# A delta-rule recurrence with a mixture-of-depths block on one core: four matmul tiles side by side, queries turned late, keys loaded once, table blocks interleaved by two

## The chip, the core and the metric

The kernel runs on one core of one Trainium2 chip. Time is device time in microseconds (us) from the launch's first to its last instruction, the median of several executions; lower is better. Five engines work beside each other, each strictly through its own list of instructions: TensorE (PE; its weight loads are PEld), VectorE (DVE), ScalarE (ACT), GpSimd (POOL) and SyncE (SP), which here only issues DMAs. An instruction that waits on one engine holds up everything behind it on that engine.

## The reference

Four batches, eight heads, 768 tokens, head dimension 48. Per head a 48x48 state is read and updated token by token (delta rule), and the heads' outputs side by side are rows of 384 numbers. Then, per batch, the 128 rows with the highest score go through a two-layer network and are added back with a gate.

```python
k_n = k / (np.linalg.norm(k, axis=-1, keepdims=True) + 1e-06)
for t in range(S):
    kt, vt, bt = (k_n[:, :, t], v[:, :, t], beta[:, :, t, None])
    y[:, :, t] = np.einsum('bhd,bhde->bhe', q[:, :, t], state)
    v_old = np.einsum('bhde,bhd->bhe', state, kt)
    state = state + bt[:, :, :, None] * np.einsum('bhd,bhe->bhde', kt, vt - v_old)
# x: (B, S, H*D)
scores = np.einsum('bsd,d->bs', x, w_gate)
out = x.copy()
for b in range(B):
    top_idx = np.argpartition(-scores[b], capacity)[:capacity]   # capacity 128
    xe = x[b, top_idx]
    ye = np.maximum(xe @ w1, 0.0) @ w2                           # 384 -> 1024 -> 384
    g = 1.0 / (1.0 + np.exp(-scores[b, top_idx]))
    out[b, top_idx] = x[b, top_idx] + g[:, None] * ye
```

## The kernel before

**Chunks.** The tokens are cut into chunks of 64, so that a chunk's 64 updates become matmuls and one triangular inverse. Batches go in two groups of two (16 heads, in 8 pairs); a group has 12 chunks, one after the other, and the two groups follow each other: 24 steps i.

**Per step.** `prep(i)` loads keys and queries, turns both on TensorE (L431), copies them out (ACT, L435), and multiplies keys by keys and keys by queries in one matmul of 128 columns (L448); ACT copies the results (L457) to `g` and `p`, and POOL masks `p` (L465). `recur(i)` is the chain through the state: `mm_r` (keys times the old state, L682), `sub` on DVE (L686), `mm_w` (inverse times right side, L694), `out_w` on ACT twice (L700), `mm_s` (new state, L708), `out_s` on ACT (L714); beside it `mm_q` (queries times state, L721), `mm_p` (L731), the copy to `x` (L737), the store to `out` (L744) and the scores (POOL L749, ACT L756).

**Per four steps.** `eliminate(e)`, e = 0 to 5, inverts the triangles of four chunks. On 128 partitions lie 128 blocks' halves: DVE turns the table in (L536), ACT takes a root (L542), DVE makes scales (L546 to L551), multiplies the table (L561), ACT copies it to PSUM (`fill`, L566), and then DVE does 29 working pairs of a product (L575) and a subtraction (L579), each step needing the one before; a closing multiplication (`final`, L585) and two transposes, `turn_out` to `tt` (L589) and `turn_back` to `g` (L594). A DMA on SP moves half of `tt` (`mv`, L600), and `join` makes the other half with small matmuls (`z` L635, `jj` L646). Only then can `mm_w` of those four steps start.

**Per batch.** `depths(b)` spreads the scores (L837), counts for each token how many are larger (compares L870 to L881, on POOL for batches 0, 1 and 3, on DVE for batch 2; count matmuls L894), picks the 128 row numbers (`choose` L913, `mm_idx` L920 in fp32), gathers the rows, and runs the two layers (L951, L965), gate (L970) and scatter (L974).

**What sets the order.** All work is given to `Plan` with an engine, an assumed duration, what it needs and a priority; `Plan` makes every engine's list from that before the program is built. Nothing is reordered on the chip. Where its plan leaves TensorE little to do, `Plan.fill` puts in a filler: two bf16 matmuls of ones (L1055) whose result nobody reads. SP's list holds all loads but a few early ones, and the stores.

Of tiles: a matmul of at most 64 rows and 64 columns takes a quarter of TensorE's array. The rows are chosen by the input's partitions (0 or 64 on), the columns by the output's. `mm_r` goes through the four combinations in the order `par_rt`; `mm_w` and `mm_q` use two of them, with the same number for rows and columns:

```python
nc.tensor.matmul(pw[half[par], a % 2, a // 2],                       # mm_w
                 lhsT=tt[half[par], ch * GP + a], rhs=x[half[par], a], ...)
y[half[rt], (2 * a + par) * D:(2 * a + par + 1) * D]                 # mm_q, output
lhsT=kq[ds[rt], a, 1, half[par]], rhs=s_old[ds[rt], a, par]          # mm_q, inputs
```

Of the kernel before, what the change touches and what calls it, by code (L numbers as in the profile page):

```python
# [20 lines left out]
class Op:  # L21
    __slots__ = ("eng", "dur", "emit", "deps", "prio", "take", "give", "lat",
                 "start", "end", "left", "users", "seq")


class Plan:
# [56 lines left out]
    def fill(self):  # L83
# [5 lines left out]
        for op in ops + [None]:  # L89
            end = op.start if op else last  # L90
            while t + 0.15 < end:
                if any(a < t < b for a, b in used):
                    t += 0.1
                    continue
                near = sum(min(y, t) - max(x, t - 3.4) for x, y in work[-40:] if y > t - 3.4)
                if near < 2.4:
                    fill = Op()
                    fill.eng, fill.start, fill.end, fill.give, fill.seq = "PE", t, t, [], -1
                    fills.append(fill)
                    work.append((t, t + 0.3))  # L100
                t += 0.3
            if op:
                work.append((op.start, op.end))
                t = max(t, op.end)
# [86 lines left out]
def kernel(  # L191
# [33 lines left out]

    nc = tc.nc
# [21 lines left out]
    SPARE = (10, 11)  # L248
# [15 lines left out]
    ring("k", 3, [GP, DP])  # L264
    ring("ks", 4, [GP, D])
    ring("q", 3, [GP, DP])
    ring("v", 3, [GP, D])
    ring("kq", 12, [GI, 2, P])
    ring("p", 12, [GP, C])
    ring("g", 2, [NB, C])  # L270
    ring("a", 1, [HC, HC])
    ring("mb", 1, [HC, HC])
    ring("tt", 2, [NB, C])
    ring("x", 2, [GB, DM // 2])
    ring("xw", 1, [GB, DM // 2])
    ring("rep", 2, [NT, P])
    ring("sel", 1, [NT, P])
    ring("cmp", 1, [22 * P], BF16)
# [3 lines left out]
    ring("oe", 1, [DM])  # L282
# [12 lines left out]
    def maker(eng):  # L295
        def add(dur, emit, deps=(), prio=0.0, take=(), give=(), lat=0.15):
            return plan.add(eng, dur, emit, deps, prio,
                            [(t[0] if isinstance(t, tuple) else t, t) for t in take],
                            give, lat)
        return add  # L300
# [3 lines left out]
    def moved(eng, dur, size, emit, deps=(), prio=0.0, take=(), give=(), lat=1.9):  # L304
# [6 lines left out]
    beta_src = beta.rearrange("(g bb) (r par) (e c half t) -> par half g e c (bb r) t",  # L311
                              bb=GB, par=2, half=2, t=HC, c=BC)

    def load_beta(eng, e):
        for par in range(2):
            for half in range(2):
                p0 = (par * 2 + half) * HC
                eng.dma_start(out=bt[p0:p0 + HC, e],
                              in_=beta_src[par, half, e // (NCH // BC), e % (NCH // BC)])
# [5 lines left out]
    tok = [sbuf(f"tok{b}", [NT, 2]) for b in range(B)]  # L325
    wg = sbuf("wg", [DM // 2])
    fold = sbuf("fold", [C])
# [4 lines left out]
    spare = w1_sb.rearrange("p t f -> p (t f)")  # L332
    w = GI * 2 * P
    rings["kq2"] = [spare[:, m * w:(m + 1) * w].rearrange("p (r o t) -> p r o t", o=2, t=P)
                    for m in range(2)]
    plan.ring("kq2", 2)
    w = GP * C
    rings["p2"] = [spare[:, 4 * w + m * w:4 * w + (m + 1) * w]
                   .rearrange("p (r t) -> p r t", t=C) for m in range(2)]
    plan.ring("p2", 2)  # L340
    rings["g2"] = [w2_sb.rearrange("p f d -> p (f d)")[:, :NB * C]
                   .rearrange("p (n t) -> p n t", t=C)]
# [8 lines left out]
    junk = sbuf("junk", [DM // 2], BF16)  # L351
    sc = [sbuf(f"sc{b}", [NCH]) for b in range(B)]
# [4 lines left out]
    def constants():  # L357
# [3 lines left out]
        for t in rings["k"][:4] + rings["q"] + rings["k"][4:]:  # L361
            nc.vector.memset(t[:, :, D:], 0.0)
        make_identity(nc, ident)
# [3 lines left out]
        load_beta(nc.gpsimd, 0)  # L367
# [8 lines left out]
        for b in range(B):  # L376
            nc.gpsimd.iota(tok[b][:, :, 0], pattern=[[P, NT]], base=b * S,
                           channel_multiplier=1, allow_small_or_imprecise_dtypes=True)
        nc.vector.tensor_tensor(out=fold, in0=ident[:, :C], in1=ident[:, C:], op=ALU.add)

    def load_w(what, t):
        if what == 0:
            step = list(moe_w_gate.ap[0])[0]
            for rt in range(2):
                nc.sync.dma_start(out=wg[half[rt]], in_=bass.AP(
                    tensor=moe_w_gate.tensor, offset=moe_w_gate.offset + 2 * D * rt * step,
                    ap=[[0, C], [4 * D * step, HP // 2], [step, 2 * D]]))
# [10 lines left out]
    par_rt = [(0, 0), (1, 1), (0, 1), (1, 0)]  # L398
    half = [slice(par * C, (par + 1) * C) for par in range(2)]
    lo = [slice(par * C, par * C + HC) for par in range(2)]  # L400
    hi = [slice(par * C + HC, (par + 1) * C) for par in range(2)]
    ds = [slice(rt * DP, rt * DP + D) for rt in range(2)]

    def load(i, nm, eng=None):
        g, c = divmod(i, NCH)
        eng = eng or nc.sync

        def emit():
            t = got(nm, i)
            for par in range(2):  # L410
                eng.dma_start(
                    out=t[half[par], :, :D],
                    in_=src[nm[0]][par, c * C:(c + 1) * C, g * GP:(g + 1) * GP])
# [4 lines left out]
    def gk(e):  # L418
        return "g2" if e == 2 else "g"

    def kk(i):
        return "kq2" if i in SPARE else "kq"

    def pk(i):
        return "p2" if i in SPARE else "p"

    def turn(i, o, nm):
# [6 lines left out]
        def out():  # L434
            nc.scalar.copy(got(kk(i), i)[:, :, o],  # L435
# [3 lines left out]
    def bank(i, w, rt):  # L439
        return got("inv", i, w, rt).rearrange("p (r o t) -> p r o t", o=2, t=C)  # L440

    def products(i, n, w, o):
# [643 lines left out]
```

## Time and profile before

| | |
|---|---|
| median of 3 runs | 365.71 us (361.34 to 366.37) |
| the profiled execution | 365.55 us |
| its span, first to last instruction | 363.7 us |
| mean granted TensorE clock | 0.809 of full |
| busy: PE / PEld / DVE / ACT / POOL | 311.0 / 267.2 / 212.5 / 168.8 / 173.4 us |
| matmul instructions | 6156 |

A busy share says how long an engine had something under way, not that it ran at its peak or that anything waited for it. The granted clock has two levels, 1.2 GHz (0.50 in the rows) and 2.4 GHz (1.00); a stretch between them was part at one and part at the other. The page's own chain of waits covers just the last 16 us, the closing of the program, so the limits are read from the engines' timelines. The three stretches used below are: up to the first `out_w`, from there to the last, and the rest.

### The profile page before, as it was taken

Reading aid. Unit: us, or ns where it says so; the run is one execution under the profiler, and the core shown is the slowest. Engines: PE = TensorE matmul, PEld = TensorE weight load, DVE = VectorE, ACT = ScalarE, POOL = GpSimd, SP = SyncE. Lnnn points to the kernel's source line nnn. Section 1 sums busy time; section 2 is a strip of 40 time slices with the busy share of each in tenths; the row PEclk is TensorE's granted clock in tenths of the full one; section 3 lists DMA queues with packets and bytes.
Section 4 is the critical chain, followed back from the end, with each engine's and each line's share of the span. In section 5 each row is a group of like instructions: output and inputs, shape, how many; then the busy total and the mean of one; then the engine's idle time right before and its main releaser. Section 6 shows DMA issues by size and latency. Waiting matters only on the chain. (4 is left out here: it accounts for less than half of the span.)

```text
span 363.7 us, 14373 instructions
## 1 busy us (share of the span) xinstructions
PE 311.0 (86%) x6156; PEld 267.2 (73%) x6156; DVE 212.5 (58%) x538; ACT 168.8 (46%) x453; POOL 173.4 (48%) x221
## 2 busy tenths in 40 slices
PE   6797679998759997998947897989999998988992
PEld 5575558887649875987837777879899787858781
DVE  5159995799918699769938897696542512301000
ACT  1476635666154585565646554443344552211121
POOL 6026426013543126334297549885694287393111
PEclk9999965799555798589968996785555999995998
DMA  9467767476453345645584845243130120111011
GB/s 120 93 132 138 136 118 125 78 137 129 74 113 81 76 98 106 128 87 118 118 208 120 198 95 98 58 83 78 42 54 23 47 48 22 14 31 22 23 22 22
DMA packets 139678, 31.92 MB, mean 88 GB/s; under 512 B 137488, under 2 KB 139040, under 8 KB 139616
## 3 DMA queue, kind: packets, MB, share of 16 engines
q1 hardware_dynamic: 134432, 28.64, 39.8%
q0 software_dynamic: 960, 1.59, 2.6%
q10 hardware_dynamic: 4224, 0.79, 1.5%
q8 instruction: 48, 0.79, 0.9%
q14 instruction: 14, 0.11, 0.1%
HBM read 22.61 MB, written 5.51 MB: 77 GB/s over the span
## 5 line engine op out<-in xcount | busy, mean ns | idle before, releaser
L575 DVE TENSOR_TENSOR tmp<-a,pa 128x30 f32<-128x30 f32 (+9 forms) x180 | 58.9, 327 | 21.2 <-ACT pa L566 15.7
L579 DVE TENSOR_TENSOR pa<-pa,tmp 128x30 f32<-128x30 f32 (+9 forms) x180 | 60.8, 338 | 6.2
L674 POOL TENSOR_TENSOR v<-v,nnT 128x384 f32<-128x384 f32 x24 | 20.8, 867 | 82.3 <-DMA v<-in_v_dram 50.7
L870 POOL TENSOR_SCALAR cmp<-rep,tok 128x256 bf16<-128x256 f32 (+5 forms) x42 | 46.5, 1119 | 7.5 <-PE inv L894 7.4
L749 POOL TENSOR_TENSOR xw<-x,wg 128x384 f32<-128x384 f32 x23 | 23.2, 1011 | 33.3 <-ACT x L737 12.6
L465 POOL TENSOR_SCALAR_AFFINE_SELECT p<-p 64x512 f32<-64x512 f32 x44 | 28.8, 654 | 18.0 <-ACT p L457 16.5
L448 PE MATMUL inv<-kq 48*64 48x128 f32 (+1 forms) x832 | 32.4, 288 | 5.6 <-ACT kq L435 2.7
L694 PE MATMUL prec<-r,tt 64*64 64x48 f32 x704 | 31.2, 245 | 4.7 <-ACT tt L651 3.0
L694 PEld LDWEIGHTS prec<-r,tt 64*64 64x64 f32 x704 | 28.0, 159 | 8.1 <-ACT tt L651 3.4
L700 ACT COPY wbd<-prec 64x384 f32<-64x384 f32 x48 | 22.7, 473 | 22.5 <-PE prec L694 17.8
L448 PEld LDWEIGHTS inv<-kq 48*64 48x64 f32 x832 | 25.2, 155 | 10.6 <-ACT p L457 3.7
L721 PE MATMUL inv<-s,kq 48*64 48x48 f32 x640 | 30.6, 258 | 1.6 <-ACT w_sb L640 1.6
L435 ACT COPY kq<-inv 128x512 f32<-128x512 f32 x44 | 24.8, 591 | 15.0 <-DMA q<-in_q_dram 8.6
L951 PEld LDWEIGHTS inv<-xeT,w_sb 128*128 128x128 f32 x192 | 26.6, 208 | 5.1 <-ACT xeT L945 1.1
L721 PEld LDWEIGHTS inv<-s,kq 48*64 48x64 f32 x640 | 28.2, 174 | 3.0 <-ACT w_sb L640 1.7
L951 PE MATMUL inv<-xeT,w_sb 128*128 128x128 f32 x192 | 27.9, 295 | 0.0
L708 PE MATMUL psta<-wbd,ks 128*48 128x96 f32 x352 | 24.2, 294 | 3.2 <-ACT wbd L700 3.2
L651 ACT COPY tt<-inv 32x256 f32<-32x256 f32 x48 | 17.3, 361 | 19.4 <-DMA tt<-tt 14.2
L686 DVE TENSOR_TENSOR r<-v,prec 128x384 f32<-128x384 f32 x22 | 12.1, 551 | 23.9 <-PE prec L682 12.7
L731 PE MATMUL inv<-wbd,p 128*64 128x96 f32 x352 | 25.1, 301 | 1.1 <-POOL p L465 1.0
L965 PE MATMUL inv<-w_sb,hT 128*128 128x384 f32 x64 | 25.4, 500 | 0.0
L708 PEld LDWEIGHTS psta<-wbd,ks 128*48 128x48 f32 x352 | 19.2, 149 | 6.4 <-ACT wbd L700 4.7
(112 smaller groups left out, 551.8 us busy)
## 6 DMA issues: line engine op xcount, KB each, us to landing
v<-in_v_dram SPq DMA_DIRECT2D x48, 96.0 KB
out_dram<-x SPq DMA_DIRECT2D x96, 48.0 KB
k<-in_k_dram SPq DMA_DIRECT2D x44, 96.0 KB
q<-in_q_dram SPq DMA_DIRECT2D x44, 96.0 KB
ks<-in_k_dram SPq DMA_DIRECT2D x44, 96.0 KB
tt<-tt SPq DMA_DIRECT2D x12, 128.0 KB
w_sb<-in_moe_w_dram SPq DMA_DIRECT2D x4, 384.0 KB
w_sb<-in_moe_w_dram SPq DMA_DIRECT2D x3, 512.0 KB
```

The costliest lines, as they stand in the source:

```text
L435: nc.scalar.copy(got(kk(i), i)[:, :, o], got("inv", i, nm).rearrange("p (r t) -> p r t", t=P))
L448: nc.tensor.matmul(bank(i, w, rt)[half[par], r, o], lhsT=kq[ds[rt], r, 0, half[par]], rhs=kq[ds[rt], r, o, half[par]], start=True, stop=True)
L465: nc.gpsimd.affine_select(out=t[half[par]], in_=t[half[par]], pattern=[[0, GP], [1, C]], base=0, channel_multiplier=-1, compare_op=ALU.is_ ...
L575: nc.vector.tensor_tensor(out=t, op=ALU.mult, in0=a[:, j + 1:, j:j + 1].to_broadcast([P, w, j]), in1=x[:, j:j + 1, :j].to_broadcast([P, w, ...
L579: nc.vector.tensor_tensor(out=x[:, j + 1:, :j], in0=x[:, j + 1:, :j], in1=t, op=ALU.subtract)
L694: nc.tensor.matmul(pw[half[par], a % 2, a // 2], lhsT=tt[half[par], ch * GP + a], rhs=x[half[par], a], start=True, stop=True)
L708: nc.tensor.matmul(psta[ds[a % 2], a // 2], lhsT=t[:, a, :D], rhs=wb[:, a].rearrange("p h d -> p (h d)"), start=(c == 0 and a < 2), stop=True,
L721: nc.tensor.matmul(y[half[rt], (2 * a + par) * D:(2 * a + par + 1) * D], lhsT=kq[ds[rt], a, 1, half[par]], rhs=s_old[ds[rt], a, par], star ...
L731: nc.tensor.matmul(y[half[a % 2], (a // 2) * 2 * D:(a // 2 + 1) * 2 * D], lhsT=t[:, a], rhs=wb[:, a].rearrange("p h d -> p (h d)"), start= ...
L870: eng.tensor_scalar(out=cmp[:, at + x * P:at + y * P], in0=rows[:, x * P:y * P], scalar1=mine, scalar2=None, op0=op)
L951: nc.tensor.matmul(got("inv", b, "h", f // 2)[:, f % 2 * CAP:(f % 2 + 1) * CAP], lhsT=w1_sb[:, t, f * P:(f + 1) * P], rhs=got("xeT", b)[:, ...
L965: nc.tensor.matmul(got("inv", b, "o")[:CAP, :DM], lhsT=got("hT", b)[:, f], rhs=w2_sb[:, f], start=(f == 0), stop=(f == KF - 1))
```

## The change

What it does, part by part:

- `mm_q` and `mm_w` go through all four combinations of row half and column half (list `four`). For that the value side puts the batch of a group, and not the parity of the head, on the partition half, and `y` is spread over two banks.
- Keys by keys (`products_g`) and keys by queries (`products_p`) become separate matmuls of 64 columns, since their outputs now lie by different bits of the head. Queries are loaded and turned later (own rings `qT`, 7, and `kT`, 12).
- `mm_s` reads the keys that were loaded for turning (ring `k`, 12): the second load of the keys (`ks`) goes. Scores and stores take whole rows of 384: one store a step for four, one score for two. All `beta` loads go to POOL, at the start.
- Tables `g` and `tt` hold two blocks interleaved, so their transposes and shift DMAs see pairs of neighbouring numbers.
- In `eliminate`, two `a` tables; for e of 1 and more the scaling runs on POOL, and the mask is applied before it (`clear`), not after it by a table.
- Compares run on DVE for batches 1 to 3; `mm_idx` is bf16 with the numbers split in three parts.
- `Plan.fill` weighs TensorE's work by a rate and fills more often: 139 fillers for 44.

```diff
+    ring("k", 12, [GP, DP])
...
+    ring("kT", 12, [GI, P])
+    ring("qT", 7, [GI, P])
...
+    ring("a", 2, [HC * HC])
+    ring("tt", 2, [NB // 2, C, 2])
...
+    four = [(0, 0), (1, 1), (0, 1), (1, 0)]
...
+    def products_g(i):
+            t = got("kT", i)
+            for k in range(2):
+                for par in range(2):
+                    for rt, bb in four:
+                        x = t[ds[rt], 2 * bb + k, half[par]]
+                        nc.tensor.matmul(small(i, "g", rt)[half[bb], k, par], lhsT=x, rhs=x,
+                                         start=True, stop=True)
...
         def mm_w():
-            for a in range(GP):
-                for par in range(2):
-                    nc.tensor.matmul(pw[half[par], a % 2, a // 2],
-                                     lhsT=tt[half[par], ch * GP + a],
-                                     rhs=x[half[par], a], start=True, stop=True)
+            for m in range(GP // 2):
+                for bb, par in four:
+                    nc.tensor.matmul(pw[half[par], bb, m], lhsT=tt[half[bb], m, par],
+                                     rhs=x[half[bb], 2 * m + par], start=True, stop=True)
...
+            for k in range(2):
+                for par in range(2):
+                    for rt, bb in four:
+                        nc.tensor.matmul(
+                            y(rt)[half[bb], k, par], lhsT=t[ds[rt], 2 * bb + k, half[par]],
+                            rhs=s_old[ds[rt], 2 * bb + k, par],
+                            start=(k == 0 and par == 0), stop=False, skip_group_check=True)
...
+        eng, on = (nc.vector, dve) if e == 0 else (nc.gpsimd, pool)
...
+        last = on(0.35, square, [s["in"]], u)
+        cl = pool(1.5, clear, [last], u)
+        s["rt"] = act(0.3, root, [last], -600)
+        s["nn"] = dve(0.85, norms, [s["rt"], N.get(("e", e - 2), {}).get("fi")], u)
+        s["sc"] = on(0.6, scales, [s["nn"]], u)
+        last = on(1.4 if e == 0 else 2.2, scale, [s["sc"], cl], u)
         last = act(1.0, fill, [last], -600, take=[("A", e)])
         for j in range(1, HC - 1):
             emit, dur = step(j)
-            last = dve(dur, emit, [last], u)
+            last = dve(dur, emit, [last, N.get(("e", e - 1), {}).get("tb")], u)
...
-        on, eng = (dve, nc.vector) if b == 2 else (pool, nc.gpsimd)
+        on, eng = (dve, nc.vector) if b >= 1 else (pool, nc.gpsimd)
...
-                if near < 2.4:
+                if near < 2.8 and (t > 3.4 or t + 0.12 < end):
```

How the lists change at two places. First DVE, where the first elimination ends (`a_100` and `a_107` its table, `g_99` and `g_106` the table of the second elimination). Before:

```order
L585 TENSOR_TENSOR a_100<-pa,mb_101 128x1024
L589 STREAM_TRANSPOSE tt_102<-a_100 128x32x32
L594 STREAM_TRANSPOSE g_98<-a_100 128x32x32
L536 STREAM_TRANSPOSE a_100<-g_99 128x1024
L538 TENSOR_SCALAR nrm<-a_100 128x32
L546 TENSOR_SCALAR nrm<-nrm 128x32
L548 RECIPROCAL bh_141<-nrm 128x32
L549 TENSOR_TENSOR bh_141<-bh_141 128x32
L550 TENSOR_TENSOR bh_141<-bh_141,bt 128x32
L551 STREAM_TRANSPOSE nnT_138<-nrm 128x32
L561 TENSOR_TENSOR a_100<-a_100,bh_141 128x1024
L563 MEMSET a_100 128x32
```

With the change:

```order
L612 TENSOR_TENSOR pa<-pa,tmp 128x3x28
L577 TENSOR_SCALAR nrm<-nrm 128x32
L579 RECIPROCAL bh_155<-nrm 128x32
L580 STREAM_TRANSPOSE nnT_152<-nrm 128x32
L608 TENSOR_TENSOR tmp<-a_107,pa 128x58
L612 TENSOR_TENSOR pa<-pa,tmp 128x2x29
L608 TENSOR_TENSOR tmp<-a_107,pa 128x30
L612 TENSOR_TENSOR pa<-pa,tmp 128x30
L618 TENSOR_TENSOR a_107<-pa,bh_154 128x16x2x32
L624 STREAM_TRANSPOSE tt_109<-a_107 128x32x16x2
L630 STREAM_TRANSPOSE g_105<-a_107 128x32x16x2
L608 TENSOR_TENSOR tmp<-a_108,pa 128x30
```

The second elimination's preparation has moved ahead of the first one's end (its transpose in stands eight instructions above the first row shown), its multiplications and the clearing have gone to POOL, and the first step of the second elimination follows `turn_back` at once.

Second SP, around the first `mv` (`tt_102` and `tt_109`). Before:

```order
L411 DMA v_73<-in_v_dram 64x8x48 x2
L411 DMA ks_66<-in_k_dram 64x8x48 x2
L411 DMA k_62<-in_k_dram 64x8x48 x2
L476 DMA w_sb<-w_sb 32x16x32 x2
L411 DMA k_63<-in_k_dram 64x8x48 x2
L600 DMA tt_102<-tt_102 32x32x32 x2
L411 DMA q_68<-in_q_dram 64x8x48 x2
L476 DMA w_sb<-w_sb 32x16x32 x2
L411 DMA q_70<-in_q_dram 64x8x48 x2
L318 DMA bt<-in_beta_dram 32x1x32 x4
```

With the change:

```order
L400 DMA w_sb<-in_moe_w_dram 128x1024 x2
L425 DMA q_74<-in_q_dram 64x8x48 x2
L425 DMA q_75<-in_q_dram 64x8x48 x2
L425 DMA q_73<-in_q_dram 64x8x48 x2
L637 DMA tt_109<-tt_109 32x16x64 x2
L422 DMA v_76<-in_v_dram 64x8x48 x2
L425 DMA k_61<-in_k_dram 64x8x48 x2
L794 DMA out_dram<-x_111 2x64x384
```

The `ks` and `bt` issues are gone from SP (208 DMAs in all for 337), the keys of twelve chunks stand ahead of all else, and weights of the network are loaded before the first `mv`.

## Rows read from the trace of the kernel before

**Rows 1.** A window of ten us: span, busy us (instructions) of each engine, granted clock, DMA share, GB/s
```profile
270.00:280.00 10.00, 10.00 (x196) 9.44 (x196) 1.35 (x4) 5.64 (x19) 4.95 (x6) 0.50 0.08 23
```
**Rows 2.** Timeline of ACT, `fill` of the first and last elimination: start, us, instruction
```profile
26.19 1.02 ACT L566 COPY pa<-a 128x1024 f32<-128x1024 f32 x1 [0.47 <-DVE a L563]
...
227.24 1.02 ACT L566 COPY pa<-a 128x1024 f32<-128x1024 f32 x1 [0.23 <-DVE a L563]
```
**Rows 3.** Timeline of DVE, between eliminations: first end, fourth end, last end
```profile
49.33 1.23 DVE L585 TENSOR_TENSOR a<-pa,mb 128x1024 f32<-128x1024 f32 x1
...
175.50 1.96 DVE L589 STREAM_TRANSPOSE tt<-a 128x1024 f32<-128x1024 f32 x1
177.32 2.14 DVE L594 STREAM_TRANSPOSE g<-a 128x1024 f32<-128x1024 f32 x1
...
179.49 1.97 DVE L536 STREAM_TRANSPOSE a<-g 128x1024 f32<-128x1024 f32 x1
...
256.07 1.23 DVE L585 TENSOR_TENSOR a<-pa,mb 128x1024 f32<-128x1024 f32 x1
```
**Rows 4.** The page's costliest groups, the two operations of the elimination's steps
```profile
L575 DVE TENSOR_TENSOR tmp<-a,pa 128x30 f32<-128x30 f32 (+9 forms) x180 | 58.9, 327 | 21.2 <-ACT pa L566 15.7
L579 DVE TENSOR_TENSOR pa<-pa,tmp 128x30 f32<-128x30 f32 (+9 forms) x180 | 60.8, 338 | 6.2
```
**Rows 5.** Waits of DVE: who waited for whom, us in total, times, longest
```profile
DVE tmp L575 <- ACT pa L566: 15.7, 5, 7.6
DVE r L686 <- PE prec L682: 12.7, 7, 3.2
```
**Rows 6.** Timeline of SP's queue around the fourth `mv`
```profile
179.55 2.30 SPq L391 DMA_DIRECT2D w_sb<-in_moe_w_dram  x2
181.95 1.37 SPq L600 DMA_DIRECT2D tt<-tt  x2
```
**Rows 7.** Timeline of ACT, `out_w`: first step, two in mid program, last step
```profile
64.11 0.96 ACT L700 COPY wbd<-prec 64x384 f32<-64x384 f32 x2
...
195.44 0.96 ACT L700 COPY wbd<-prec 64x384 f32<-64x384 f32 x2
...
214.79 0.96 ACT L700 COPY wbd<-prec 64x384 f32<-64x384 f32 x2 [1.17 <-PE prec L694]
...
296.94 0.96 ACT L700 COPY wbd<-prec 64x384 f32<-64x384 f32 x2 [1.05 <-PE prec L694]
```
**Rows 8.** Timeline of PE at full clock: `mm_q`, `mm_r`, `mm_w`
```profile
166.59 1.10 PE L721 MATMUL inv<-s,kq 48*64 48x48 f32 x32
...
171.92 0.68 PE L682 MATMUL prec<-s,w_sb 48*64 48x48 f32 x32
...
173.55 1.13 PE L694 MATMUL prec<-r,tt 64*64 64x48 f32 x32
```
**Rows 9.** Timeline of PE at half clock: `mm_r`, `mm_q`, three fillers
```profile
260.38 1.10 PE L682 MATMUL prec<-s,kq 48*64 48x48 f32 x32 [0.58 <-ACT s L714]
261.27 1.91 PE L721 MATMUL inv<-s,kq 48*64 48x48 f32 x32
263.11 0.82 PE L1055 MATMUL psta<-warm 128*128 128x128 bf16 x6
```
**Rows 10.** Timeline of PE at full clock, products of 128 columns
```profile
29.28 1.10 PE L448 MATMUL inv<-kq 48*64 48x128 f32 x32
```
**Rows 11.** Lines of PE by form, 20 to 35 us, products of 64 columns
```profile
L448 PE MATMUL inv<-kq 48*64 48x64 f32 x64 | 1.5, 225 | 0.0
```
**Rows 12.** Lines by form, whole span: `mm_idx`, and POOL's `beta` loads
```profile
L920 PE MATMUL inv<-tok,sel 128*128 128x2 f32 x48 | 9.4, 323 | 0.0
...
L318 POOL DMA_DIRECT2D bt<-in_beta_dram x4 | 2.6, 653 | 0.3 <-issue 0.3
```
**Rows 13.** Timeline of DVE, last count of batch 3
```profile
328.94 0.16 DVE L906 TENSOR_TENSOR count<-count,inv 128x4 f32<-128x4 f32 x1 [10.91 <-PE inv L894]
```
**Rows 14.** Waits of POOL: for the values' load
```profile
POOL v L674 <- DMA v<-in_v_dram: 50.7, 12, 9.0
```

More of the change, by code (lines that the diff above doesn't have):

```diff
@@ L324 @@
     tri = sbuf("tri", [P])
-    tok = [sbuf(f"tok{b}", [NT, 2]) for b in range(B)]
-    wg = sbuf("wg", [DM // 2])
-    fold = sbuf("fold", [C])
+    own = [sbuf(f"own{b}", [NT]) for b in range(B)]
+    tok = [sbuf(f"tok{b}", [NT, 2, 3], BF16) for b in range(B)]
+    part = sbuf("part", [NT])
+    both = [sbuf(f"both{b}", [2]) for b in range(2)]
+    wg = sbuf("wg", [DM])
     warm = sbuf("warm", [P], BF16)
@@ L509, in prep @@
[L509 removed]
+        for w, v, made, deps, rate in (
+                ("g", u, (products_g, split_g), [n["ek"], N[e * BC].get("g")], 1.2),
+                ("w", u + 31, (products_p, split_p), [n["ek"], n["eq"]], 1.2)):
             keys = [("inv", i, w, rt) for rt in range(2)]
[L511 to L521 removed]
@@ L522, in prep @@
-        n["mp"] = pool(1.4, mask_p(i), [n["e", 1, 0], n["e", 1, 1]], 10 * i - 10)
-        done = [n["e", 0, 0], n["e", 0, 1]]
-        if first:
-            n["sh"] = dve(0.85, shift0(i), done, u)
+            n[w] = pe(0.52, made[0](i), deps, v, rate=rate,
+                      take=keys + ([("p", i)] if w == "w" else
+                                   [gk(e)] * (i % BC == 0)))
+            for rt in range(2):
+                n[w, rt] = act(0.37, made[1](i, rt), [n[w], n.get((w, 0))], v,
+                               give=[keys[rt]])
@@ L602, in eliminate @@
-        s["in"] = dve(2.2, turn_in, [N[i].get("sh") for i in range(e * BC, (e + 1) * BC)],
+            left, right = lower(got("tt", e), slice(0, NB // 2))
+            for x in range(2):
+                nc.sync.dma_start(out=left[lo[x]], in_=right[lo[x]])
+        s["in"] = dve(1.3, turn_in, [N[i].get("sh") for i in range(e * BC, (e + 1) * BC)],
                       u, take=[("a", e)])
-        s["rt"] = act(0.3, root, [s["in"]], -600)
-        s["sc"] = dve(1.0, scales, [s["rt"], N.get(("beta", e)),
-                                    N.get(("e", e - 2), {}).get("mb")], u)
@@ L765, in recur @@
+        r["w"] = pe(0.52, mm_w, [x, n["ej"], s_mv(e), o.get("w0"), o.get("w1")], u, rate=1.5,
+                    give=[("tt", e)] + ([("v", i)] if c == 0 else []))
+        for par in range(2):
+            r[f"w{par}"] = act(0.45, out_w(par),
+                               [r["w"], prev2.get("p"), prev2.get("s")], u)
+        ready = [r["w0"], r["w1"]]
         if c < NCH - 1:
-            n["ls"] = moved(sp, 1.3, 1.15, load(i, "ks"), prio=10 * i - 24, take=[("ks", i)])
-        r["vh"] = pool(1.05, vh, [n["lv"], N["e", e]["sc"]], u - 8)
@@ L791, in recur @@
+        xo = None
+        for rt in range(2):
+            xo = act(0.37, out_x(rt), [r["p"], xo], 10 * i + 8, take=[("x", i)] * (rt == 0),
+                     give=[yk[rt]])
         how = dve if i == NU - 1 else act
```

580 lines of the change are left out of this document (283 added, 297 removed).

## The prediction, made before the changed kernel ran

> **What bounds the kernel now.** I read the page's busy shares first and trusted none: TensorE is under way 86% of the span, but a mean granted clock of 0.809 says that much of that is slow running. The windows show it best: from 270 to 280 us TensorE is busy 10.00 of 10 us at a clock of 0.50, the lower of its two levels, while DVE has 1.35 us of work [rows 1]. There TensorE is the limit, and slow. Earlier it is not alone. The timelines cut the span in three by `out_w` [rows 7]: 64.1 us to the first, 232.8 us to the last (296.94), 66.8 us for what is left.
>
> In the middle stretch DVE's eliminations set the pace. The first `fill` starts at 26.19 us, the sixth at 227.24 [rows 2]: (227.24 - 26.19)/5 = 40.2 us each. The steps' own two operations take (58.9 + 60.8)/6 = 20.0 us of that [rows 4]. The rest is the end of one elimination and the preparation of the next: `final` 1.23, the transposes 1.96, 2.14 and 1.97 us [rows 3], a scaling of the size of `final`, small operations, and waits: 15.7/5 = 3.1 us for each `fill`, and 12.7 us in all for `mm_r` [rows 5]. The last elimination ends at 256.07 [rows 3], and the last `out_w` comes 40.9 us after that, through the slow window. Between eliminations the steps can go much faster: (214.79 - 195.44)/3 = 6.45 us each [rows 7]. So there are two limits, DVE's chain up to 256 us and TensorE's list from there on, and the low clock sharpens the second.
>
> **The change, part by part.**
>
> *Matmul tiles.* `mm_r` and `mm_q` have the same shape and number, 32 instructions of 48x48. `mm_r` goes through four tiles and takes 0.68 us at full clock; `mm_q` uses two and takes 1.10, `mm_w` with two 1.13 [rows 8]. At half clock it is 1.10 against 1.91 [rows 9]. I price the new `mm_q` and `mm_w` as `mm_r`: 22 x 0.42 + 24 x 0.45 = 20 us less of TensorE at full clock; at half clock `mm_q` alone gives 22 x 0.81 = 18. The lower bound of the gain is nothing. The Trainium skill, "TensorE: Matmul & The Clock Gate", Part 3, "What overlaps and what doesn't", says that a weight load overlaps running matmuls only where the row group differs. By that rule alone `mm_q`, which already alternates row halves, would gain nothing and the sum would lose these 20 us. The trace speaks against it, since `mm_r` and `mm_q` both alternate rows and differ by 0.42 us; I keep it as a rival.
>
> *Products.* One set of 128 columns takes 1.10 us [rows 10], a set of 64 columns 1.5/2 = 0.75 [rows 11]. Twenty steps (the first four were split already) now do two: 20 x 0.40 = 8 us more.
>
> *Fillers.* 95 more, each a third of 0.82 us at half clock [rows 9], so about 0.27, or half of it at full: 13 to 26 us more of TensorE. At full clock the three terms give -20 + 8 + 13 = +1 us: TensorE's list gets no shorter. What it can gain is the clock. The window that is 10.00 us busy at 0.50 [rows 1] says that small matmuls, however tightly packed, need not bring the high level; the change adds 128-column bf16 work among them. The Trainium skill, same page, "What's actually happening", has the clock follow how busy TensorE has been; by that, filling a busy list changes nothing and only costs. This row disagrees with it. I take part of the gain: the high level most of the time, not always.
>
> *Eliminations.* Scaling and the small multiplications leave DVE for five of six: about 2.0 us each (`final`'s 1.23 for the large one, the rest for the small). Three transposes of pairs: between 1.23 (a plain operation of that size) and today's 2.0 [rows 3]; I take 1.4, so 3 x 0.6 = 1.8 us. The `fill` of the next elimination can run under `turn_out` and `turn_back`, since its table is ready by then: 3.1 us of wait go. Together 6.9, which makes 33.3 us; unchanged would be 40.2. What is late next is `sub`: it stands at fixed places among the elimination's steps, and now TensorE must bring four `mm_r` within 33 us instead of 40. Four steps at 6.45 are 26 us, but they share TensorE with the next chunks' turns and products. I take 36, nearer the lower end. POOL now has a link of this chain: its scaling stands behind `vh`, which waits for loads of the values, 50.7 us in twelve waits, up to 9.0 [rows 14]. With the preparation moved ahead by some 9 us (fourteen of the steps' operations at 20.0/58 = 0.34, `final` and two transposes) that is covered, except for the longest; if it isn't, each elimination pays some 4 us.
>
> *SP's list.* 129 issues fewer of about 0.65 us (a pair takes 1.37 [rows 6]). The fourth `turn_out` ends at 177.46 [rows 3], and its `mv` is issued at 181.95 behind weights [rows 6]: 4.5 us in which `tt` lies ready. I take 3 us off each such wait. Stores and keys become fewer without anyone waiting for them; that costs nothing as long as twelve chunks of keys come early, and they stand first in the list.
>
> *Start.* POOL issues 24 `beta` loads at 0.653 us, 15.7 us, ahead of everything else [rows 12], and the first `clear` stands behind them. I leave the first `fill` at about 27 us. DVE does the second elimination's transpose in and scales before the first `final`, some 2.5 us. First `final`: 49.33 + 2.5 = 52; the first `out_w`, with 3 us less at SP and a shorter transpose, at 63.
>
> *End.* `mm_idx` falls from 9.4/4 = 2.35 us [rows 12] to six bf16 matmuls, 0.82 at half clock as the fillers of that number [rows 9]; two of the four lie in the last stretch: -3 us. Batch 3's count waits 10.91 us [rows 13] for compares on POOL that DVE does now. TensorE had other work in most of that, so I take 5. With a steadier clock 3 more: 66.8 - 11 = 56 us.
>
> **The sum.** The last `final` at 52 + 5 x 36 = 232 us. From it to the last `out_w`: not 40.9 but 33. The other bound is 30: the hand-over as at the first elimination, 64.11 - 49.33 = 14.8, less the 4.5 us at SP, and three steps of 6.45. That gives 265, and 56 more give a span of 321. The profiled execution was 365.55 us with a span of 363.7, so 1.9 us lie around it: **323 us**. That execution lies at the median, 365.71.
>
> **Rivals.**
>
> (a) *DVE's floor.* Everything keeps pace: 33 us an elimination, 30 us after the last, 50 at the end: 52 + 165 + 30 + 50 + 2 = 299 us. For it: the wait for `fill` goes by construction. Against: the waits for `mm_r` [rows 5] grow when the pace rises.
>
> (b) *TensorE's list binds and the clock stays as it is.* Then only its work counts: -30 for tiles (between 20 and 37), +8 for products, +20 for fillers, -8 for `mm_idx` and the end, -5 at SP: 365.5 - 15 = 350 us. For it: rows 1. Against: a denser list has reached the high level in this trace with the same steps [rows 8].
>
> (c) *The slower side: four tiles don't run side by side for `mm_w` and `mm_q`, and TensorE binds.* Their inputs are now read with a step of two numbers (`tt`) or spread over two banks (`y`), which no row shows. Then the 30 us of (b) are missing: 380 us, 4% slower. It decides as soon as their 32 instructions take over 1 us at full clock. This is also where the weight-load rule above would lead.
>
> (d) *It doesn't do what it says at DVE:* POOL's link comes late by 4 us in each elimination and transposes stay at 2 us; 40 us each as before, the rest as forecast: 323 + 20 = 343; with the clock of (b) as well, about 362, no change.
>
> **Chances.** The forecast, 308 to 338 us: 0.47. (a), below 308: 0.17. (b) and the first of (d), 338 to 358: 0.20. No change, mainly (d) with (b): 0.09. (c): 0.07. Two per cent, 358.4 to 373 us, is about what a measurement can tell here (three runs spread over 1.4%). So faster 0.84, same 0.09, slower 0.07. The range from 292 to 355 leaves out about 0.04 below and 0.16 above.
>
> **What would show it.** Tiles: `mm_w` and `mm_q` at 0.65 to 0.7 us at full clock. Eliminations: `fill` to `fill` 33 to 38 us, DVE's wait for `fill` near nothing, transposes at 1.2 to 1.5. Clock: a mean of 0.88 or more, and no window busy 10 of 10 at 0.50. SP: `mv` issued within 2 us of `turn_out`. End: under 60 us from the last `out_w`. The prediction is wrong if the clock stays near 0.81, if DVE's waits for `mm_r` rise above 25 us in all, or if POOL is named as releaser of the steps.

## The result, and the profile after

The changed kernel takes **352.82 us** in the median of four executions (347.34 to 362.11), the kernel before 365.6 beside it: a ratio of 0.951 (95% interval 0.939 to 0.963), some 5% faster. Two controls later gave 349.06 and 353.93 us, ratios 0.963 (0.949 to 0.977) and 0.965 (0.946 to 0.985). The forecast was 323 us; the range (292 to 355) holds the median, but less than half of the forecast gain came. The same program takes longer in executions with a lower granted clock, so ratios compare the faster executions of either kernel, and the profile below is that of the second control (timed at 347.44 us, mean clock 0.831), not that of the execution profiled first (362.11 us, 0.796).

Timeline of ScalarE, changed kernel: start, us, and the operation. First and sixth `fill` (L599) and first and last `out_w` (L746), which answer to [rows 2, 7].

```profile
25.07 1.02 ACT L599 COPY pa<-a 128x1024 f32<-128x1024 f32 x1 [4.10 <-DVE a L596]
...
65.27 0.96 ACT L746 COPY wbd<-prec 64x384 f32<-64x384 f32 x2 [2.17 <-PE prec L741]
...
201.80 1.02 ACT L599 COPY pa<-a 128x1024 f32<-128x1024 f32 x1 [1.47 <-POOL a L596]
...
283.60 0.96 ACT L746 COPY wbd<-prec 64x384 f32<-64x384 f32 x2 [0.39 <-PE prec L741]
```

Timeline of VectorE, changed kernel: first and last `final` and the two transposes behind the first, to be read beside [rows 3].

```profile
50.19 1.23 DVE L618 TENSOR_TENSOR a<-pa,bh 128x1024 f32<-128x1024 f32 x1
51.45 1.25 DVE L624 STREAM_TRANSPOSE tt<-a 128x1024 f32<-128x1024 f32 x1
52.62 1.20 DVE L630 STREAM_TRANSPOSE g<-a 128x1024 f32<-128x1024 f32 x1
...
228.73 1.23 DVE L618 TENSOR_TENSOR a<-pa,bh 128x1024 f32<-128x1024 f32 x1
```

From `fill` to `fill` it is (201.80 - 25.07)/5 = 35.3 us instead of 40.2. Set against the forecast, with a later version (the last experiment, early queries with six buffers for v) in the last column:

| us | forecast | the change | early queries, six buffers |
|---|---|---|---|
| first `final` | 52 | 50.2 | 48.8 |
| last `final` | 232 | 228.7 | 232.2 |
| last `out_w` | 265 | 283.6 | 269.0 |
| end of the span | 321 | 345.7 | 331.2 |

Up to the last `final` the forecast is 3 us too long. From there to the last `out_w` 54.9 us pass instead of 33, and then 62.1 instead of 56. These two make the miss: -3.3 + 21.9 + 6.1 = 24.7 us.

I call the stretch from the last `fill` to the last `out_w` the **tail**. Its windows row (us, then busy time and instructions of PE, PEld, DVE, ACT and POOL, then the granted clock, the DMA share and GB/s), first of the kernel before:

```profile
227.24:296.94 69.70, 66.98 (x1492) 60.18 (x1491) 36.42 (x98) 30.23 (x83) 45.54 (x55) 0.67 0.25 53
```

and of the change:

```profile
201.80:283.60 81.80, 74.70 (x2020) 60.99 (x2022) 43.10 (x120) 45.81 (x117) 50.63 (x66) 0.81 0.29 69
```

The tail became 12 us longer though the clock in it is higher. Busy time by clock, an estimate of the work as it would be at full clock, is 67.0 x 0.67 = 44.9 us before and 74.7 x 0.81 = 60.5 now. The same program's tail in the execution profiled first, and in the first control:

```profile
204.96:298.43 93.47, 86.42 (x2020) 70.47 (x2022) 42.72 (x120) 45.89 (x118) 50.60 (x66) 0.65 0.26 61
202.72:281.35 78.63, 68.84 (x1994) 55.20 (x1990) 42.23 (x120) 45.56 (x117) 51.15 (x66) 0.89 0.31 72
```

There the estimate is 56.2 and 61.3 us, so it is good to some 5 us, and the tail's length moves by 15 us from execution to execution of one program. What came in stands in the groups of TensorE in this window of the change (busy us, mean ns | idle before):

```profile
L472 PE MATMUL inv<-qT,kT 48*64 48x64 f32 x288 | 7.5, 242 | 0.5 <-ACT qT L447 0.4
L443 PE MATMUL inv<-ident,q 128*128 128x128 f32 x36 | 7.0, 328 | 0.0
L1104 PE MATMUL psta<-warm 128*128 128x128 bf16 x48 | 6.9, 263 | 0.0
```

Nine products of queries and keys and nine turns of queries are there: (7.5 + 7.0) x 0.81 = 11.7 us at full clock. In the tail of the kernel before no row of L448 or L431 exists: its queries were done beside the eliminations. Fillers were x6 there, 0.8 us, and are 6.9 us now, 5.6 at full clock. Together that is about the difference; what else came in and went out nearly cancels.

VectorE's waits, changed kernel (us in total, times, longest), beside [rows 5]:

```profile
DVE r L730 <- PE prec L725: 26.5, 11, 7.3
DVE tmp L608 <- ACT pa L599: 13.3, 6, 5.1
```

The wait for `fill` stayed nearly what it was, 13.3 us instead of 15.7. A piece of the chain of waits, changed kernel (start, us, what), shows where the longest of these waits, 5.1 us, comes from:

```profile
159.43 0.50 SPq L422
159.92 0.04 issue
159.97 6.10 DMA v<-in_v_dram
...
166.23 0.06 POOL v L715
...
167.01 0.25 POOL bh L584
167.26 0.07 issue
167.33 0.26 POOL bh L585
167.59 0.07 issue
167.66 1.92 POOL a L594
```

GpSimd's scaling of the table (L584 to L594) stands in its list behind a `vh` (L715, the scaling of v), and that waits for a load of v, which takes 6.10 us.

### The profile page after: what moved, and what is told of

Read it like the earlier page. It is cut to its first block, busy times and chain, and to the rows that moved or that the text cites. A ratio compares the mean times of both kernels' runs of the same rounds, so it can differ in the third digit from the quotient of the medians.

```text
span 360.4 us, 15833 instructions
## 1 busy us (share of the span) xinstructions
PE 306.2 (85%) x6962; PEld 253.5 (70%) x6962; DVE 211.3 (59%) x595; ACT 168.7 (47%) x431; POOL 152.8 (42%) x222
## 4 chain that ended last, share of the span: by engine, by line
PE 58%; DMA 11%; POOL 10%; DVE 7%; ACT 5%; issue 5%; SPq 1%; POOLq 1%; DVEq 0%; ACTq 0%
DMA v<-in_v_dram 7%; PE inv L443 5%; PE inv L683 5%; PE inv L781 5%; PE inv L1001 5%; PE psta L1104 5%; PE inv L671 5%; PE inv L1015 4%; PE psta L754 4%; POOL bt L334 4%; PE inv L472 4%; PE prec L741 3%; PE inv L462 3%; PE prec L725 3%; PE inv L770 3%
## 5 line engine op out<-in xcount | busy, mean ns | idle before, releaser
L715 POOL TENSOR_TENSOR v<-v,nnT 128x384 f32<-128x384 f32 x24 | 20.8, 868 | 61.8 <-DMA v<-in_v_dram 36.1
L730 DVE TENSOR_TENSOR r<-v,prec 128x384 f32<-128x384 f32 x22 | 12.1, 550 | 50.9 <-PE prec L725 43.2
L1104 PE MATMUL psta<-warm 128*128 128x128 bf16 x278 | 35.7, 266 | 3.8 <-DVE psta L377 3.8
L781 PEld LDWEIGHTS inv<-wbd,p 128*64 128x64 f32 x384 | 23.1, 177 | 11.5 <-POOL p L495 9.0
L746 ACT COPY wbd<-prec 64x384 f32<-64x384 f32 x48 | 22.7, 473 | 16.8 <-PE prec L741 9.9
L754 PE MATMUL psta<-wbd,k 128*48 128x96 f32 x352 | 24.3, 294 | 6.6 <-ACT wbd L746 6.6
L1104 PEld LDWEIGHTS <-warm 128*128 128x128 bf16 x278 | 21.6, 116 | 8.8 <-issue 3.7
L754 PEld LDWEIGHTS psta<-wbd,k 128*48 128x48 f32 x352 | 19.2, 149 | 9.4 <-ACT wbd L746 9.0
L462 PE MATMUL inv<-kT 48*64 48x64 f32 x768 | 23.3, 254 | 2.0 <-ACT g L479 1.4
L486 ACT COPY p<-inv 128x256 f32<-128x256 f32 x48 | 15.9, 374 | 17.3 <-PE inv L472 17.1
L443 PE MATMUL inv<-ident,k 128*128 128x128 f32 x96 | 17.5, 325 | 7.0 <-ACT g L479 4.3
L443 PE MATMUL inv<-ident,q 128*128 128x128 f32 x96 | 20.0, 350 | 4.0 <-DMA q<-in_q_dram 3.9
L462 PEld LDWEIGHTS inv<-kT 48*64 48x64 f32 x768 | 19.0, 160 | 6.0 <-ACT g L479 2.6
```

The costliest lines, as they stand in the source:

```text
L443: nc.tensor.transpose(ps[:, r * P:(r + 1) * P], x[:, 2 * r:2 * r + 2].rearrange("p b d -> p (b d)"), ident)
L462: nc.tensor.matmul(small(i, "g", rt)[half[bb], k, par], lhsT=x, rhs=x, start=True, stop=True)
L746: nc.scalar.copy(wb[half[par], :, par].rearrange("p (b m) d -> p b m d", b=2), pw[half[par]])
L754: nc.tensor.matmul(psta[ds[a % 2], a // 2], lhsT=t[:, a, :D], rhs=wb[:, a].rearrange("p h d -> p (h d)"), start=(c == 0 and a < 2), stop=True,
L781: nc.tensor.matmul(y(rt)[half[bb], k].rearrange("p b d -> p (b d)"), lhsT=t[:, a], rhs=wb[:, a].rearrange("p h d -> p (h d)"), start=(c == ...
L1104: nc.tensor.matmul(pfull[:, GI * 2 * D:], lhsT=warm, rhs=warm, start=False, stop=True, skip_group_check=True)
```

## The experiments

Each edit is made on the changed kernel. Runs named together ran beside the same runs of the kernel before.

**Control, tiles and fillers** (kernel before: 367.12 us, 358.87 to 372.61).

> The changed kernel once more, as the control for the other kernels of this round. Its first profile showed TensorE at the lower clock from 224 to 282 us and the last out_w at 298 us. Clock theory: another execution has the low stretch elsewhere or shorter, and its time goes with the mean granted clock: 344 to 348 us where that is 0.83 or more, 355 to 362 where it is 0.80. Theory of the list (the steps after the last elimination are held by the length of TensorE's list and its waits, whatever the clock): the stretch from the last final to the last out_w stays near 62 us.

349.06 us (345.17 to 357.38). The time went with the mean clock, as the first theory has it: 345.17 us at 0.850, 357.38 at 0.801. From the last `final` to the last `out_w` the profiled execution has

```profile
228.80:281.35 52.55, 45.35 (x1296) 36.03 (x1290) 20.12 (x52) 28.92 (x77) 35.55 (x45) 0.91 0.27 68
```

That is not the 62 us of the second theory, but even at a clock of 0.91 it is 20 us over the forecast 33.

*Two tiles at a time.* Same instructions, lists and tiles, but two opposite tiles first and then the other two:

```diff
-            for m in range(GP // 2):
-                for bb, par in four:
+            for two in (((0, 0), (1, 1)), ((0, 1), (1, 0))):
+                for m in range(GP // 2):
+                    for bb, par in two:        # mm_q likewise
```

> mm_w and mm_q in another order: first all matmuls of the tiles (0,0) and (1,1), then all of (0,1) and (1,0), so that only two tiles are next to each other, as in the kernel before. Same instructions, same results. If side by side is what makes them fast, their 32 instructions take 1.0 to 1.1 us instead of 0.70 at full clock, and the kernel is slower by 10 to 20 us (TensorE's list counts), or by under 4 us (it does not count for most of the program). If the order of tiles is not what counts, 0.70 us stays.

367.81 us (352.82 to 371.83) against 349.06: slower in the median, by how much is unsure, since one of its four executions lies among the control's and the clocks differ. What the order costs TensorE can be read without the sum. Timeline of TensorE, this experiment, a stretch at full clock:

```profile
73.64 0.91 PE L772 MATMUL inv<-s,qT 48*64 48x48 f32 x32
75.07 0.97 PE L742 MATMUL prec<-r,tt 64*64 64x48 f32 x32
```

and the change:

```profile
74.70 0.65 PE L770 MATMUL inv<-s,qT 48*64 48x48 f32 x32
75.99 0.70 PE L741 MATMUL prec<-r,tt 64*64 64x48 f32 x32
```

So four tiles in turn save about 0.26 us on such a set of 32 at full clock; there are 46. Rows alternate from each instruction to the next in both orders. The Trainium skill, "TensorE: Matmul & The Clock Gate", Part 3, "What overlaps and what doesn't", makes the overlap of a weight load depend on the row group alone; by that the two would be equal, and these rows disagree.

*The fillers' old rule* (`if near < 2.4` with a coarser step: 134 filler matmuls instead of 278) and *many more* (782):

```diff
-                if near < 2.8 and (t > 3.4 or t + 0.12 < end):
+                if near < 4.6 and (t > 3.4 or t + 0.12 < end):
```

> The change with the filler rule of the kernel before: 67 fillers instead of 139, all else the same lists. Clock theory: a lower mean clock (under 0.79 where the control has 0.83) and 8 to 15 us slower. Theory of the list: 144 filler matmuls at 0.14 to 0.27 us less, 20 to 39 us of TensorE's time, so 10 us or more faster.

> The change with the threshold of its filler rule at 4.6 instead of 2.8: 391 fillers instead of 139, all else the same lists. Clock theory: mean clock 0.9 or more, no long stretch at the lower level, steps after the last elimination at 6.5 to 8 us each instead of 12, 15 to 30 us faster than the control. Theory of the list: 504 more filler matmuls of 0.14 us, 70 us more on TensorE, 20 us or more slower.

Old rule: 346.81 us (342.89 to 358.8), not told apart from the control, so neither theory of it came in. Many: 364.27 us (362.98 to 365.85), slower by 15 us, where the theory of the list had 20 or more. The windows of the kernel with many fillers, the eliminations and its tail:

```profile
64.00:203.00 139.00, 123.21 (x3746) 104.70 (x3744) 101.53 (x258) 78.48 (x208) 51.99 (x68) 0.94 0.41 88
203.44:294.22 90.78, 83.06 (x2050) 66.62 (x2043) 41.30 (x120) 45.63 (x118) 50.32 (x66) 0.77 0.26 61
```

A clock of 0.94 over the eliminations (0.81 in the change) did not bring the last `fill` forward: 203.44 against 201.80. But 504 more filler matmuls take TensorE's time as well, so what the clock alone is worth there is not shown. The tail became longer still.

**GpSimd's link, late queries, compares** (kernel before: 367.4 us, 362.81 to 375.0).

*Scaling ahead of `vh`.* In the finished plan, where `vh` stands directly ahead of the scaling, it is put behind it; the other four lists are the same.

```diff
+                if what == "scales" and last.emit.__name__ == "vh":
+                    late = last
+                elif what == "scale" and late:
+                    at = o.start + 0.01
+                    if all(u.start > at for u in late.users):
+                        late.start = at
...
```

> The changed kernel with one thing moved: in GpSimd's list, at four of the five eliminations that it scales, the scaling of v that stands directly ahead of the elimination's scaling is put behind it; no other list changes. In the control run of the changed kernel (349.1 us) that scaling of v waits for v's load (6.2 to 6.4 us each in the chain of waits), the elimination's scaling stands behind it, and `fill` comes 1 to 2 us after VectorE is free. Theory POOL link: `fill` comes 1 to 2 us earlier at four eliminations, 35.5 us from fill to fill become 34 to 34.5, the last fill falls from 202.7 to 196 to 199, and the whole becomes 342 to 346. Rival, TensorE's list: what VectorE gains it waits for again at the next `sub`; fills and the end within 2 us of the control, 347 to 351. A v that comes 2 us later on GpSimd could also hold a `sub`: then up to 3 us slower.

350.21 us (342.54 to 353.86), ratio 0.938 (0.930 to 0.946); the expectation had 342 to 346. The last `fill` came at 193.91, 8 us earlier than in the change, a little better than forecast, and VectorE's wait for `fill` fell from 13.3 us to

```profile
DVE tmp L623 <- ACT pa L614: 4.8, 4, 1.9
```

The link is thus shown as what delays `fill`. What it is worth in time stays open: the ratio is lower than either control's, but those ran beside other runs of the kernel before. The profiled execution shows no gain, with a tail of 94.5 us at a clock of 0.68; but the change itself has one of 93.47 at 0.65 above, so that tail need not come from the exchange.

*Most of the late query matmuls left out.*

```diff
-            for r in range(GI):
+            for r in range(1 if nm == "q" and i >= 18 else GI):   # and in products_p
```

> The changed kernel, all lists in the same order, leaving out three quarters of the matmuls of the last six units' query work: of the turn of the queries only one matmul of four, of the products of queries and keys 8 of 32 (their results are then not those of the reference). In the control the stretch from 235 us to the last out_w (281) holds 5.2 us of these products and 3.2 us of these turns. Theory late queries: they stand in TensorE's list between the last steps, so the stretch from the last fill to the last out_w falls from 78.6 us by 5 to 7, and the whole from 349 to 342 to 344. Rival, the steps wait for other engines (VectorE's compares, ScalarE's copies): TensorE only waits longer, the stretch falls by under 2 us, the whole is 347 to 350. Rival, the clock: with less work the granted clock of the stretch falls (0.89 in the control) and the time stays or grows.

354.35 us (350.48 to 356.65), ratio 0.963: no gain. Its tail:

```profile
198.28:288.11 89.83, 84.87 (x1838) 67.27 (x1836) 42.69 (x120) 45.88 (x118) 50.53 (x66) 0.59 0.27 63
```

The work did fall, to 84.87 x 0.59 = 50.1 us at full clock, but the clock was lower too, as the rival of the clock has it. That the missing matmuls lowered it is not shown, since with all of them in its lists the change had 0.65 in one execution and 0.89 in another. The test doesn't refute late queries either: the copies, masks and waits around the missing matmuls were still in the lists.

*The second batch's compares issued twice*, and *compares back on GpSimd*:

```diff
-                    if y > x:
+                    for _ in range((y > x) * (1 + (b == 1))):
-        on, eng = (dve, nc.vector) if b >= 1 else (pool, nc.gpsimd)
+        on, eng = (dve, nc.vector) if b == 2 else (pool, nc.gpsimd)
```

> The changed kernel, all lists in the same order, the comparisons of the second batch (14 on VectorE in 235 to 281 us, 6.9 us in all, new there with the change) each issued twice; the results are the same. Theory compares in the chain: they stand ahead of two of the last `sub`s and of the counts for which TensorE's list waits, so all or most of what they take is on the path: the last out_w comes 5 to 7 us later, the whole 354 to 357. Rival, TensorE's list or the late queries: VectorE is busy 16 of 46 us there, the second half of each pair falls into its idle time, the last out_w moves by under 2 us, the whole stays at 347 to 351.

> The changed kernel with one part undone: the comparisons of the second batch back on GpSimd (VectorE keeps those of the third, as before the change, and of the fourth); TensorE's list is planned anew by it. On GpSimd one 128x640 comparison takes 2.5 us in the control, on VectorE 0.62. Theory compares in the chain: VectorE's lists of the last steps are free, steps of 12 and 16 us fall to some 8, the last out_w from 281 to 272 to 276; what GpSimd now does longer (some 15 us for the batch) delays the second batch's gather but lies beside the layers of the first: the whole 341 to 346. Rival: GpSimd's weighing and masks of the last steps stand behind the slow comparisons, the last steps wait for GpSimd instead and the whole is 349 to 358.

Twice: 359.21 us (350.83 to 368.1), ratio 0.964 (0.954 to 0.974): not told apart. Its last two steps took 17.5 and 17.2 us against 12.7 and 13.6 in the change, but at clocks of 0.65 and 0.50 against 0.87, so the doubling can't be separated from the clock. On GpSimd: 375.43 us (371.98 to 380.46), ratio 1.024 (1.017 to 1.031), slower than the kernel before and outside both expectations. The edit does more than the expectation says: `b == 2` leaves VectorE only the third batch, so the fourth batch's compares go back to GpSimd as well as the second's, and the plan made anew has 330 filler matmuls instead of 278. The rival's mechanism is there for the second: in the last steps TensorE waits for GpSimd's masks, which stand behind the slow compares (kernel with the compares back on GpSimd, waits of 264 to 300 us):

```profile
ACT wbd L746 <- PE inv L781: 9.6, 1, 9.6
PEld inv L781 <- POOL p L495: 6.3, 1, 6.3
```

The fourth's come behind the last `out_w`, where 70.4 us pass instead of 62.1. The 2.5 us in the expectation are two instructions' time; of one size, 128x768, a compare takes 2.21 us on GpSimd and 0.61 on VectorE in the control. Moving the compares of both batches to VectorE was thus worth having; the share of each is not separated.

**Early queries** (kernel before: 370.74 us, 360.33 to 374.77). Nothing is left out; the planner ranks the queries' loads, turns and products 15 us more urgent:

```diff
+            if any(name in ("q", "qT", "p") for name, _ in op.take):
+                op.prio -= 15
```

> The changed kernel once more, unaltered, as the control for the three that run beside it: 345 to 353 us, 4 to 5% under the kernel before, as in its first control (349.1).

353.93 us (347.44 to 365.98), just over the expected 353.

> The changed kernel with one number in the planner: the loads, turns and products of the queries get a rank 15 us more urgent, so that TensorE's list holds none of them between the last four steps any more (there were four turns and five products); buffers, fillers' rule and everything else unchanged. Theory late work: in the control's tail, from the last fill to the last out_w, TensorE has 61 us of work at full clock (68.8 busy at 0.89) against 45 before the change (67.0 at 0.67); the late queries are 12 of these 16. Taken out, the last four steps go at 6 to 8 us each, the tail falls by 8 to 12 us; what comes earlier costs 0 to 4 us at the eliminations: the whole 338 to 345. Rival, total work: TensorE's list is the limit throughout, and work moved forward delays the eliminations' `sub`s as much as it spares at the end: the last fill comes 6 to 10 us later, the whole is 346 to 353. Rival, the clock: the tail gets shorter lists but falls to 0.5, as in the experiment that left three quarters of the late queries out (tail 89.8 us at 0.59): 347 to 356.

**335.75 us** (329.58 to 343.02): its slowest execution is faster than the control's fastest.

> As the experiment with the earlier queries, and in addition the fillers by the rule of the kernel before (60 pairs instead of 126). Fillers alone moved the time by at most 1% (346.8 against 349.1). Theory late work: 336 to 344 us, the fillers bring or cost 3 us. Rival, the clock: with fewer fillers the tail runs at 0.5 to 0.7 and the whole is 346 to 356.

> As the one before, and in addition the elimination's scaling ahead of the scaling of v in GpSimd's list where they stood the other way round (at three eliminations here). Theory POOL link: the last fill 4 to 8 us earlier than in the kernel without it, the whole 330 to 340 us. Rival: what is gained at the eliminations falls into the tail's low clock, as in the experiment with this exchange alone (last fill 8.8 us earlier, tail 94.5 us at 0.68 instead of 78.6 at 0.89): within 3 us of the kernel without it.

344.48 us (337.71 to 345.5) and 343.1 us (341.44 to 346.44), both faster than the control and, in the median, slower than the early version with the change's fillers. Their mean clocks lay at 0.755 to 0.809 and 0.761 to 0.792, that of the version with more fillers at 0.808 to 0.887. The exchange at GpSimd adds nothing that could be told apart, with the last `fill` at 200.07 instead of 202.81.

The old rule of the fillers was run without and with the earlier queries, and the two kernels differ in that rank alone. The stretch from the last `final` to the last `out_w` in each, and its groups of query products and query turns on TensorE, first without:

```profile
224.50:277.55 53.05, 49.05 (x1272) 39.07 (x1268) 19.96 (x52) 29.08 (x77) 35.20 (x45) 0.78 0.27 67
L464 PE MATMUL inv<-qT,kT 48*64 48x64 f32 x208 | 6.2, 266 | 0.0
L435 PE MATMUL inv<-ident,q 128*128 128x128 f32 x24 | 5.3, 360 | 0.9 <-ACT tt L681 0.7 <-DVE count L948 0.3
```

and with them, where no turn is left:

```profile
233.09:272.58 39.49, 37.39 (x940) 30.88 (x932) 16.95 (x48) 19.31 (x50) 30.51 (x38) 0.64 0.22 63
L466 PE MATMUL inv<-qT,kT 48*64 48x64 f32 x38 | 1.2, 224 | 0.0
```

The stretch fell by 13.6 us at a lower clock and with the same five steps in it. So neither the clock nor the change's fillers made it long. Of the span only 3.2 us of that were left in these two executions (347.0 and 343.8 us): the last `final` came 8.6 us later with the query work ahead of it, and the end took 1.8 us more. With the change's own fillers it came 3.5 us later (table).

Two last runs (kernel before: 367.39 us, 361.77 to 372.01): the early version again, and the same with `ring("v", 6, ...)` for `ring("v", 4, ...)`.

> The version with the earlier queries and the change's own fillers once more, unaltered (335.75 us, control beside it 353.9). If the gain is the list's, it comes back: 330 to 340, 7 to 10% under the kernel before. Rival, chance of the clock: 342 to 352, as the two versions with fewer fillers (344.5 and 343.1).

> The same with six buffers for v instead of four, so that SyncE can issue v's loads earlier and GpSimd's scaling, which stands behind the scaling of v, waits less for them (waits of 6 us for v's load stand in the chain of waits ahead of three of the scalings). Theory POOL link: from fill to fill 1 to 2 us less (34.6 in the run with four buffers), the last fill at 189 to 194 instead of 197.6, the whole 326 to 336. Rival: SyncE waits for other things ahead of v in its list (stores, keys), or VectorE's `sub`s take back what the fill gains: within 3 us of the version with four.

**336.32 us** (332.65 to 348.57), ratio 0.918 (0.909 to 0.927), and **334.65 us** (332.11 to 338.48), ratio 0.916 (0.907 to 0.925). The change did not run beside these two, but both intervals lie below all three of the change's. The gain of the earlier queries came back as expected. Six buffers move nothing that could be told apart: the last `fill` was at 203.76, not before 194. The tail of that kernel, and in it the stretch from the last `final` to the last `out_w`:

```profile
203.76:268.96 65.20, 60.05 (x1799) 49.80 (x1801) 43.33 (x121) 39.24 (x103) 45.31 (x58) 0.87 0.27 68
232.24:268.96 36.72, 34.86 (x995) 28.87 (x995) 19.75 (x52) 21.16 (x56) 29.58 (x37) 0.81 0.21 61
```

The tail takes 65.2 us instead of 81.8, with 60.05 x 0.87 = 52.2 us of work instead of 60.5. That this is not the clock alone, the versions with fewer fillers show: theirs were 69.8 and 69.7 us long at 0.74, a lower clock than the control's 0.81.

## Why the prediction was wrong, step by step

- **Tiles: right.** At full clock most sets of `mm_w` take 0.70 us, and the quickest of `mm_q` 0.65, near `mm_r`'s 0.68; rival (c) fell. Other sets of `mm_q` take up to 0.99.
- **Products and fillers: right.** A set of 64 columns takes 0.66 to 1.01 us at full clock (0.75 taken). Fillers went from 10.6 to 35.6 us, +25, within 13 to 26. TensorE's whole work at full clock is 295.6 x 0.831 = 246 us against 311.0 x 0.809 = 252: the list got hardly shorter, as the sum said.
- **Eliminations: right in size, wrong in one part.** 35.3 us (36 forecast), transposes 1.25, 1.20 and 1.24 (1.4). But the wait for `fill` was to go and did not; for the last five `fill`s the table now comes from GpSimd, in the longest wait behind v's load. I had taken that link as covered but for the longest wait. With `vh` out of its way the wait fell to 4.8 us.
- **SyncE: right but for the first.** At the second elimination `turn_out` ends at 91.35, and `mv` is issued at 92.74; the later ones follow within 1.6 us. The first waits from 52.70 to 56.74, behind six loads of queries, and the first `out_w` comes at 65.3, not 63.
- **"From it to the last `out_w`: not 40.9 but 33": this step failed.** I took the steps' pace from before [rows 7] and left out what "queries turned late" puts between them. In this stretch of 54.9 us (40.9 before) stand seven products and six turns of queries, 10.7 us, and 4.7 us of fillers, where before stood none and 0.8; and five steps where there were four. Ranking the queries earlier, with nothing left out and five steps still, brought the stretch to 268.96 - 232.24 = 36.7 us, near the 33. With the fillers' old rule the rank alone took it from 53.05 to 39.49. This is more than the 8 to 10 us of query work that left it. What else in the steps got shorter stays open, and part of it is work that now stands ahead of the last `final`.
- **Clock: wrong.** A mean of 0.88 was forecast, 0.831 measured (0.778 to 0.865 over all executions of the change), and the window from 230 to 240 is still 9.87 us busy at 0.50. A higher mean (0.891) bought with many fillers came with a slower kernel. With early queries the change's own fillers do pay, in the median: 344.5 us with 120 filler matmuls, 335.75 with 252. But the clock is not what made the stretch above long: at 0.91 it still took 52.55 us.
- **End: half at best.** 62.1 us at a clock of 0.97, and 66.6 at 0.88 in the first control, not 56 (before: 66.8 at 0.91). In the first of these `mm_idx` gave 3.1 us (4.0 to 0.9) and the layers 3.9 (53.3 to 49.4). The compares' 5 came only as 2.8 us less idle time, and 4.1 us of other matmuls (counts, spreads, last products) moved behind the last `out_w`.
- **Rivals.** (b) gave 350, the nearest number, by another reason, so that is luck: it has TensorE's list bind everywhere, but in the 201.80 us up to the last `fill` `sub` waits only 13.8 us for `mm_r`, and the eliminations got faster as forecast. (a) and (d) fell with 35.3 us an elimination, neither 33 nor 40. Two of the prediction's own signs of failure are there. GpSimd releases `fill`, and the waits for `mm_r` are 26.5 us, over 25, though they vary (21.1 and 43.2 in the two other executions) and nearly half of them lie behind the last `fill`.

## What to carry to other kernels

When a change makes work late, put it by name into the last stretch, where nothing covers it any more, before taking that stretch's length from the old profile. A stretch's busy time by its granted clock tells roughly whether work came in or only the clock changed. Before a stretch of one profile is put down to an edit, look how far that stretch moves between executions of one program: the tail here moved by 15 us. A link moved to an idle engine waits for whatever stands ahead of it in that engine's list, loads included.

## What the runs showed of the hardware

TensorE's granted clock did not follow its busy share. One program, the change, was busy 68.84 of 78.63 us of its tail at 0.89 in one execution and 86.42 of 93.47 us at 0.65 in another. In the tail with three quarters of the late query matmuls gone it was busy 84.87 of 89.83 us and got 0.59; with many fillers, over the eliminations, 123.21 of 139 us and got 0.94. The Trainium skill, "TensorE: Matmul & The Clock Gate", "What's actually happening", has the clock set by how busy the engine has been; by busy time as the profile counts it, these rows disagree. A low clock itself makes the same matmuls busy for longer (`mm_r` 1.10 us instead of 0.68 [rows 8, 9]), so a busy share near one is no sign of a high clock. What decides the clock, these runs don't tell.
